# Batch 0's first two chunks store their score blocks unturned, and later chunks fetch and turn them

## The chip, the cores and the metric

One core of a Trainium2 chip runs the whole program. The metric is the device time of one execution in microseconds (us). The kernel before takes 2275.74 us, the median of three runs (2274.81 to 2275.78).

## The reference, cut to what matters

For each of 8 batches (3200 rows; `u` and `v` are 3200x256, `z` is 3200x64, all float32):

```python
scores = (1.0 / S) * np.matmul(z, z.transpose(0, 2, 1))
attn = np.maximum(scores, 0.0) ** 2
x = u * np.matmul(attn, v)
# xp: x with 4 rows of zeros ahead; K = 5
for k in range(K):
    gate_pre += conv_w[k] * xp[:, k:k + S, :]
out = (sigmoid(gate_pre) * (x @ w_val)) @ w_out
```

The matrix of scores is z times its own transpose, so it is symmetric: a block computed once is, turned over its diagonal, also the block at the mirrored place.

## The kernel before, in words

The 3200 rows of a batch are 25 tiles of 128. Queries go in 7 chunks `c` of 4, 4, 4, 4, 3, 3, 3 tiles (the last batch differs a little), and keys in 13 pairs of tiles `i` (the last pair is one tile). A step is one chunk against one pair, so a batch has 91 steps. `place[b, c, i]` says at which of a chunk's 13 places a pair is taken.

**One block.** A float32 product is made of three passes over a high and a low part (`hi`, `lo`, both fp32r). For a computed block TensorE (PE) makes the scores into a PSUM tile `s` of which there are two (`scores`, six 64-row matmuls, two at a time, recorded at L394). ScalarE (ACT) then does Relu (L589), Square (L590) and the cast to `ah` (L592, the high part), and VectorE (DVE) the rest `al` = a - ah (L598). PE multiplies `ah` and `al` with the values `v_hl` into `acc` (`attend`, L394 and L642). All this is written three steps ahead (`AHEAD = 3`): in step s PE makes the scores for step s + 3 in its middle, and ACT and DVE make the weights of s + 3.

**Mirrored blocks.** `keeps(b, c, g)` says whether the block of query chunk c and key chunk g > c is kept. If so, DVE turns it in 32x32 squares (`turn`, L468) into a tile `turned`, and `keep` stores it with four transfers into the DRAM tensor `mir`. When chunk g comes to the pairs of chunk c, `m_fetch` (L505) brings the block back into one of four buffers `m`, and only cast and rest are left: no scores, no Relu, no Square. In batch 0 chunk 0 is not kept at all, and chunk 1 only for g of 5 and 6. In the other batches every block with c < g is kept. `MIRRORED_AT` spreads the fetched pairs over the places of a chunk by their number.

**Order of the work.** Nothing is scheduled by the compiler: each engine takes its instructions in the order in which the Python loop over steps writes them. `at_step(s, fn, ...)` puts loads and side work (convolution, gate, value and out projections, conversion of the float64 weights) at a step. SyncE's queue (SP) issues all transfers in the same written order, and an issue that has to wait holds up those behind it. The transfers take eight semaphores (`DMAHW0` to `DMAHW7`) in turn, and a transfer waits until the one that had its semaphore before, eight issues earlier, has landed. Batch 0 starts with nothing on the core: while its chunk 0 is computed, SP loads `z`, all of `v`, the weights and `u` for batch 0 (`z_load`, `v_load0`, `v_load_chunk`, `u_load`).

**Buffers.** `a` has two tiles, `m` four, `turned` two, `v_raw` two. The float64 conversions (`convert_conv`, `convert`) take their scratch from `m` in the first chunks.

Of the kernel before, what the change touches and what calls it, by code (L numbers as in the profile page):

```python
# [7 lines left out]
F32 = mybir.dt.float32  # L8
# [4 lines left out]
P = 128  # L13
# [4 lines left out]
def attn_glu_kernel(  # L18
# [66 lines left out]

    def from_float64(dst, rest, raw, split, **kw):

        lo_w, hi_w = raw[..., 0], raw[..., 1]
        cols = 1
        for n in dst.shape[1:]:  # L90
            cols *= n
        ws = [sb.tile([P, 2, cols], U32, name=f"cv_words{i}", tag="m", bufs=4) for i in range(2)]
        ex, sc, mant, frac = (w[:, i, :].rearrange(split, **kw) for w in ws for i in range(2))
        ts, tt = nc.vector.tensor_scalar, nc.vector.tensor_tensor
        yield
        ts(ex, hi_w, 20, 0x7FF, op0=ALU.logical_shift_right, op1=ALU.bitwise_and)
# [24 lines left out]
        yield
        tt(dst, mant.bitcast(F32), rest, op=ALU.add)
# [20 lines left out]
    def convert(name):  # L143
        hi = const.tile([P, DH, D], F32R, name=f"w_{name}_hi")
        lo = const.tile([P, DH, D], F32R, name=f"w_{name}_lo")
        both = sb.tile([P, 2, DH, D], F32, name="w_f32", tag="m", bufs=4)
        wf, rest = both[:, 0], both[:, 1]
        yield from from_float64(wf, rest, w_raw[name], "p (h d) -> p h d", d=D)
        if name == "out":
# [137 lines left out]
    def keeps(b, c, g):  # L287

        return c < g and (b > 0 or c > 1 or (c == 1 and g >= 5))

# [168 lines left out]
    def turn(b, c, i, a):  # L459

        w = all_sizes[b][c] * P
        for j, g, t, m in runs(b, i):
            if keeps(b, c, g):
                size = all_sizes[b][g]
# [8 lines left out]
        if two_pairs(b, c) and i == own(b, c, 0):  # L473
# [20 lines left out]
    def m_fetch(b, c, i):  # L494
# [40 lines left out]
    def second_block(a, hi, lo, s):  # L535
        each = a.shape[1] // 2
        for j in range(2):
# [7 lines left out]
            rest(lo[:, x], a[:, x], hi[:, x])  # L545

    def weights_of(b, c, i):

# [5 lines left out]
        if halves(b, c, i) or split(b, c, i):  # L554
# [22 lines left out]
            return rests  # L577
        if mirrored(b, c, i):
            a = m_in.pop((b, c, i))[:, : n * w].rearrange("p (a j x) -> p a j x", a=P // BLK, j=n)
            hi, lo = (x.rearrange("p (j a x) -> p a j x", a=P // BLK, j=n) for x in (hi, lo))  # L580
        else:
            s = st_.pop((b, c, i))
            a = sb.tile([P, 2 * CW], F32, name="a", bufs=2)[:, : n * w]
            each = n * w // 2
            if b == c == 0 and i < 2:
                at[b, c, i] = (ah, al)
                first_block(a, hi, lo, s) if i == 0 else second_block(a, hi, lo, s)
                return lambda: None
            nc.scalar.activation(a.rearrange("p (j x) -> p j x", j=2), s[:, :, :each], AF.Relu, scale=scale)  # L589
            nc.scalar.activation(a, a, AF.Square)  # L590
        if cast_on_scalar(b, c, i):
# [5 lines left out]
        def rest():  # L597
# [4 lines left out]
            if not mirrored(b, c, i):  # L602
                if c == 1 and two_pairs(b, c) and i == own(b, c, 0) and place[b, c, i] == 0:
                    return lambda: turn(b, c, i, a)
                turn(b, c, i, a)

# [415 lines left out]
    for b in range(B):  # L1022
        for c in range(n_chunks):
# [39 lines left out]
            for i in range(NP):  # L1063
                if mirrored(b, c, i) or halves(b, c, i) or split(b, c, i):
                    at_step(s0 + place[b, c, i] - AHEAD - FETCH, m_fetch, b, c, i, first=True)
        if b == 0:
# [7 lines left out]
        else:  # L1074
            s1 = start(b - 1, n_chunks - 1)
            for i, p in enumerate(V_HIGH[b > 1]):
                at_step(s1 + p, v_high, b, i)
                at_step(s1 + p + 1, v_low, b, i)
            for p, tiles in V_LOAD[b > 1]:
                at_step(s1 + p, v_load, b, tiles)  # L1080
# [10 lines left out]
    with tc.manual_schedule():  # L1091
# [7 lines left out]
        for s in range(min(todo), END + 1):  # L1099
# [169 lines left out]
```

## Time and profile before

| what | before |
|---|---|
| median of 3 runs | 2275.74 us |
| span of the profiled execution (its own time has no row) | 2270.9 us |
| around the span, by the median | 4.8 us |
| PE, PEld busy | 2263.4, 2017.6 us |
| DVE, ACT busy | 1846.1, 1758.2 us |
| share of 16 DMA engines, queue q1 | 70.3% |
| chunk 0 of batch 0, 0 to 55.4 us | 55.4 us |
| chunks 1 to 6 of batch 0 | 46.6, 49.3, 46.2, 36.2, 33.6, 36.1 us |
| chunks 1 to 6 of batch 2 | 45.9, 44.3, 43.4, 33.9, 31.6, 34.3 us |

A chunk is taken from one `x<-acc,ut` product (L672), which ends a chunk's attention, to the next. Lines of a timeline give start, duration, engine, line of the kernel, operation, output<-inputs, and in brackets how long the engine was idle before and what released it. PE's matmuls overlap, so a group's own duration is longer than the distance to the next group's start; distances between starts are what PE takes.

### The profile page before, as it was taken

The numbers are of one execution on the slowest core, as the hardware profiler recorded it, in microseconds if no ns is written. First come the engines' busy times: TensorE is split into PE (matmuls) and PEld (weight loads), VectorE is DVE, ScalarE is ACT, GpSimd is POOL, SyncE is SP. The second block draws the span as 40 slices with busy tenths as digits, with TensorE's granted clock in tenths as the row PEclk, the third lists the DMA queues.
The fourth block names the chain that finished last, engine by engine and source line by source line (L and its number), as shares of the span: only waits on it lengthen the run. The fifth ranks groups of instructions, "written<-read, shape, count | busy, mean of one in ns | idle before, by whom it ended". The sixth has DMA issues, their size and how long they took to land.

```text
span 2270.9 us, 52418 instructions
## 1 busy us (share of the span) xinstructions
PE 2263.4 (100%) x21229; PEld 2017.6 (89%) x21229; DVE 1846.1 (81%) x2427; ACT 1758.2 (77%) x2326; POOL 65.3 (3%) x110
## 2 busy tenths in 40 slices
PE   9999999999999999999999999999999999999999
PEld 7889988899888998889988899888998889998889
DVE  7877798887988778887798878888788887788776
ACT  8987789766987669876698776986769876697755
POOL 0000000000000000000000000000000000000000
PEclk9999999999999999999999999999999999999999
DMA  5255776778667786677867778677687786877753
GB/s 119 44 119 117 178 172 156 178 168 212 157 159 177 164 221 160 157 174 167 211 157 168 179 169 195 157 177 175 159 200 164 182 173 156 197 170 177 194 145 97
DMA packets 691651, 374.96 MB, mean 165 GB/s; under 512 B 399312, under 2 KB 662992, under 8 KB 691408
## 3 DMA queue, kind: packets, MB, share of 16 engines
q1 hardware_dynamic: 690208, 371.35, 70.3%
q8 instruction: 166, 2.72, 0.5%
q14 instruction: 77, 0.63, 0.1%
q10 hardware_dynamic: 1200, 0.26, 0.1%
HBM read 205.86 MB, written 165.61 MB: 164 GB/s over the span
## 4 chain that ended last, share of the span: by engine, by line
PE 99%; DVE 0%; issue 0%; ACT 0%; DVEq 0%
PE acc L394 68%; PE s L394 11%; PE misc L394 10%; PE acc L642 8%; PE misc L834 1%; PE misc L758 1%; PE misc L401 0%; PE acc L834 0%; PE s L758 0%; DVE x L672 0%; DVE gvl L780 0%; DVE zhl L244 0%; DVE turned L478 0%; DVE a L527 0%; PE misc L214 0%
## 5 line engine op out<-in xcount | busy, mean ns | idle before, releaser
L394 PE MATMUL acc<-ah,v_hl 64*128 64x512 f32 (+1 forms) x9800 | 1543.2, 370 | 0.5 <-DVE ah L529 0.5
L394 PEld LDWEIGHTS acc<-ah,v_hl 64*128 64x128 f32 x9800 | 927.3, 185 | 120.6 <-issue 1.4
L394 PE MATMUL acc<-al,v_hl 64*128 64x512 f32 (+1 forms) x4900 | 921.6, 369 | 0.0
L598 DVE TENSOR_TENSOR al<-a,ah 128x1024 fp32r<-128x1024 f32 (+4 forms) x386 | 421.7, 1093 | 225.0 <-ACT ah L592 218.4
L394 PEld LDWEIGHTS acc<-al,v_hl 64*128 64x128 f32 x4900 | 469.2, 185 | 60.0 <-DVE al L516 0.9
L589 ACT ACTIVATE a<-s 128x1024 f32<-128x1024 f32 (+4 forms) x386 | 354.1, 917 | 160.9 <-PE s L394 147.9
L590 ACT ACTIVATE a<-a 128x1024 f32<-128x1024 f32 (+4 forms) x386 | 370.2, 959 | 12.2
L592 ACT CAST ah<-m 128x768 fp32r<-128x768 f32 (+2 forms) x303 | 269.1, 892 | 127.4 <-DMA m<-mir 52.4
L592 ACT CAST ah<-a 128x1024 fp32r<-128x1024 f32 (+3 forms) x351 | 334.5, 953 | 11.5
L598 DVE TENSOR_TENSOR al<-m,ah 128x768 fp32r<-128x768 f32 (+2 forms) x303 | 308.0, 1019 | 40.3 <-ACT ah L592 39.3
L468 DVE STREAM_TRANSPOSE turned<-a 128x1024 f32<-128x1024 f32 (+3 forms) x318 | 319.5, 1010 | 1.3 <-DMA mir<-turned 0.7
L713 DVE SCALAR_TENSOR_TENSOR gate<-x,cw,gate 128x512 f32<-128x512 f32 (+2 forms) x448 | 304.5, 680 | 4.4 <-ACT gate L711 0.3
L394 PE MATMUL s<-zq,zhl 64*128 64x512 f32 (+3 forms) x1722 | 231.9, 372 | 0.0
L394 PEld LDWEIGHTS s<-zq,zhl 64*128 64x128 f32 x1722 | 161.3, 185 | 23.1
L642 PE MATMUL acc<-ah,v_hl 128*128 128x384 f32 (+2 forms) x700 | 177.8, 332 | 0.2 <-DVE x L672 0.2
L672 DVE TENSOR_TENSOR x<-acc,ut 128x512 f32<-128x512 f32 (+2 forms) x112 | 65.8, 628 | 85.0 <-PE acc L394 55.4
L642 PEld LDWEIGHTS acc<-ah,v_hl 128*128 128x128 f32 x700 | 124.7, 188 | 4.6 <-issue 1.8
L642 PE MATMUL acc<-al,v_hl 128*128 128x384 f32 (+2 forms) x350 | 115.6, 330 | 0.0
L718 ACT ACTIVATE gate<-gate 128x512 f32<-128x512 f32 (+2 forms) x112 | 65.6, 585 | 58.2 <-DVE gate L713 58.1
L775 ACT CAST gvh<-gv 128x512 fp32r<-128x512 f32 (+2 forms) x112 | 64.0, 572 | 47.6 <-DVE gv L771 47.5
L771 DVE TENSOR_TENSOR gv<-misc,gate 128x512 f32<-128x512 f32 (+1 forms) x110 | 69.5, 632 | 15.1 <-PE misc L394 8.1
L711 ACT ACTIVATE gate<-x,cw 128x512 f32<-128x512 f32 (+2 forms) x111 | 74.8, 674 | 2.6 <-DVE x L672 2.6
(139 smaller groups left out, 1978.1 us busy)
## 6 DMA issues: line engine op xcount, KB each, us to landing
m<-mir SPq DMA_DIRECT2D x191, 384.0 KB, 5.1
mir<-turned SPq DMA_DIRECT2D x340, 192.0 KB, 3.3
mir<-turned SPq DMA_DIRECT2D x188, 256.0 KB, 4.0
m<-mir SPq DMA_DIRECT2D x94, 512.0 KB, 5.2
u_raw<-in_u_dram SPq DMA_DIRECT2D x264, 64.0 KB, 3.7
v_raw<-in_v_dram SPq DMA_DIRECT2D x116, 128.0 KB, 4.7
mir<-turned SPq DMA_DIRECT2D x84, 144.0 KB, 2.5
out_dram<-ob SPq DMA_DIRECT2D x92, 128.0 KB, 2.8
```

Of the source, the lines that this page charges most:

```text
L394: ins = nc.tensor.matmul(out_, st[r], mv[r], start=first, stop=last)
L468: nc.vector.transpose(into[:, t : t + m], a[:, j * w : (j + m) * w].rearrange("p (t m x) -> p t m x", t=m, x=BLK))
L589: nc.scalar.activation(a.rearrange("p (j x) -> p j x", j=2), s[:, :, :each], AF.Relu, scale=scale)
L590: nc.scalar.activation(a, a, AF.Square)
L592: nc.scalar.copy(hi, a)
L598: nc.vector.tensor_tensor(lo, a, f32(hi), op=ALU.subtract)
L642: nc.tensor.matmul(out_, st, mv, start=first, stop=last)
L672: nc.vector.tensor_tensor(x[:, h, HALO : HALO + w], accs[b, c][h][:, :w], ut[b, c][:, h, :w], op=ALU.mult)
L711: (first or nc.scalar.mul)(g, tap, cw[:, h, 0:1])
L713: nc.vector.scalar_tensor_tensor(g, tap, cw[:, h, k : k + 1], g, op0=ALU.mult, op1=ALU.add)
L718: nc.scalar.activation(g, g, AF.Sigmoid)
L771: nc.vector.tensor_tensor(gv[:, :w], pvs[b, c][e][:, :w], gates[b, c][:, e, :w], op=ALU.mult)
```

## The change

In batch 0 the blocks of chunks 0 and 1 are kept too (`keeps` is now `c < g` everywhere). They are not turned when they are made. Their `a` tile comes from the four `m` buffers in place of the two `a` buffers, the Relu writes it in strips of 64 columns of both tiles, and `keep_as_is` stores it from there with one transfer per key chunk into a DRAM tensor `raw`, in pieces of 512 or 256 bytes. A later chunk fetches such a block one step earlier than other blocks, with four transfers of 128 or 96 KB, and `turn_in` turns it on DVE one step ahead of the cast, into an `a` tile. With this, batch 0's chunks have the same fetched pairs as the other batches' (10 more blocks of 4 tiles' width, 8 more of 3), and `place` follows `MIRRORED_AT` for these numbers. Blocks of chunk 1 with g of 5 and 6, turned before they were stored until now, are stored unturned too. The two large conversions take their scratch from `v_raw` and `turned` in place of `m`; the conversion of the convolution's weights keeps its scratch in `m`. The loads and casts of batch 1's values go to the places that the other batches use.

```diff
-    def from_float64(dst, rest, raw, split, **kw):
+    def from_float64(dst, rest, raw, split, ws=None, **kw):
...
-        ws = [sb.tile([P, 2, cols], U32, name=f"cv_words{i}", tag="m", bufs=4) for i in range(2)]
+        ws = ws or [sb.tile([P, 2, cols], U32, name=f"cv_words{i}", tag="m", bufs=4) for i in range(2)]
...
-        both = sb.tile([P, 2, DH, D], F32, name="w_f32", tag="m", bufs=4)
+        both = sb.tile([P, 2, DH, D], F32, name="w_f32", tag="v_raw", bufs=2)
...
+        words = sb.tile([P, 2, 2, DH * D], U32, name="cv_words", tag="turned", bufs=2)
...
-        return c < g and (b > 0 or c > 1 or (c == 1 and g >= 5))
+        return c < g
+
+    def as_is(b, c):
+
+        return b == 0 and c < 2
...
-            if keeps(b, c, g):
+            if keeps(b, c, g) and as_is(b, c):
+                to_keep.append((b, c, g, a, j, t, m))
+            elif keeps(b, c, g):
...
+    def keep_as_is(b, c, g, a, j, t, m):
+
+        y = 2 * BLK
+        if (b, c, g) not in mirror:
+            mirror[b, c, g] = dram.tile([P, 2 * P // BLK, all_sizes[b][g] * y], F32, name=f"raw{c}_{g}", bufs=1)
+        nc.sync.dma_start(
+            mirror[b, c, g][:, :, t * y : (t + m) * y],
+            a.rearrange("p (z x) -> p z x", z=2 * P // BLK)[:, :, j * y : (j + m) * y],
+        )
...
+        if turns_in(b, c, i):
+            raw = mirror[b, i // 2, c].rearrange("(k r) (a h) x -> h a r k x", r=BLK, h=2)[i % 2]
+            into = mt[:, : P // BLK * n * y].rearrange("p (k x) -> p k x", k=P // BLK)
+            for a in range(P // BLK):
+                nc.sync.dma_start(into[a * BLK : (a + 1) * BLK], raw[a])
+            return
...
+    def turn_in(b, c, i):
+
+        n, w = pairs[i][1], all_sizes[b][c] * P
+        raw = m_in.pop((b, c, i))[:, : n * w]
+        a = turned_in[b, c, i] = sb.tile([P, 2 * CW], F32, name="a", bufs=2)[:, : n * w]
+        nc.vector.transpose(
+            a.rearrange("p (t m r) -> p t m r", t=2, r=BLK), raw.rearrange("p (m t r) -> p t m r", t=2, r=BLK)
+        )
...
-            a = sb.tile([P, 2 * CW], F32, name="a", bufs=2)[:, : n * w]
...
+            kept = as_is(b, c) and keeps(b, c, all_homes[b][k][0])
+            a = sb.tile([P, 2 * CW], F32, name="a", **(dict(tag="m", bufs=4) if kept else dict(bufs=2)))[:, : n * w]
...
+            if kept and n == 2:
+                raw, a, hi, lo = a, *by_strips(a, hi, lo)
+                s = s[:, :, :w].rearrange("p j (z x) -> p j z x", x=2 * BLK)
+                nc.scalar.activation(a, s, AF.Relu, scale=scale)
+                nc.scalar.activation(raw, raw, AF.Square)
...
-                    at_step(s0 + place[b, c, i] - AHEAD - FETCH, m_fetch, b, c, i, first=True)
+                    at_step(s0 + place[b, c, i] - AHEAD - FETCH - turns_in(b, c, i), m_fetch, b, c, i, first=True)
...
-            for i, p in enumerate(V_HIGH[b > 1]):
+            for i, p in enumerate(V_HIGH[1]):
...
-            for p, tiles in V_LOAD[b > 1]:
+            for p, tiles in V_LOAD[1]:
...
+            if ahead and s + AHEAD + 1 < N and turns_in(*steps[s + AHEAD + 1]):
+                turn_in(*steps[s + AHEAD + 1])
```

Where the instructions stand now is shown at two places. The first is SP's queue while chunk 0 of batch 0 is computed; `v_raws` are values, `z_raw` the rows of z, and the brackets name what an issue waits for. Before:

```order
L331 DMA v_raws<-in_v_dram 32x4x256 [waits DMAHW5_49]
L173 DMA z_raw<-in_z_dram 32x12x32 [waits DMAHW6_49,DVE_49]
L173 DMA z_raw<-in_z_dram 32x12x32 [waits DMAHW7_49]
L173 DMA z_raw<-in_z_dram 32x12x32 [waits DMAHW0_49]
L173 DMA z_raw<-in_z_dram 32x12x32 [waits DMAHW1_49]
L331 DMA v_raws<-in_v_dram 32x3x256 [waits DMAHW2_49]
L331 DMA v_raws<-in_v_dram 32x3x256 [waits DMAHW3_49]
```

And after the change, from the same transfer on (`raw_1`, `raw_2` are the stores of pairs 2, 3 and 4):

```order
L337 DMA v_raws<-in_v_dram 32x4x256 [waits DMAHW5_49]
L494 DMA raw_1_308<-a 1024x1x128 [waits DMAHW6_49,Activation_49]
L494 DMA raw_1_308<-a 1024x1x128 [waits DMAHW7_49,Activation_49]
L494 DMA raw_2_360<-a 1024x1x128 [waits DMAHW0_49,Activation_49]
L175 DMA z_raw<-in_z_dram 32x12x32 [waits DMAHW1_49,DVE_49]
L175 DMA z_raw<-in_z_dram 32x12x32 [waits DMAHW2_49]
L175 DMA z_raw<-in_z_dram 32x12x32 [waits DMAHW3_49]
L175 DMA z_raw<-in_z_dram 32x12x32 [waits DMAHW4_49]
L337 DMA v_raws<-in_v_dram 32x3x256 [waits DMAHW5_49]
L337 DMA v_raws<-in_v_dram 32x3x256 [waits DMAHW6_49]
L337 DMA v_raws<-in_v_dram 32x3x256 [waits DMAHW7_49]
L337 DMA v_raws<-in_v_dram 32x3x256 [waits DMAHW0_49]
```

Three stores now stand ahead of the rows of z for chunk 6, and the last three issues of this piece wait for the stores' own semaphores 6, 7 and 0 again.

The second place is ACT's queue in the same stretch: the Relu, Square and cast of pairs 5, 6 and 7. Before:

```order
L589 ACTIVATE a<-s 128x1024 [waits DVE_49,PE_49]
L590 ACTIVATE a<-a 128x1024 [waits Activation_49]
L592 CAST ah<-a 128x1024 [waits Activation_49]
L239 CAST zhl_396<-zz 128x384 [waits DVE_49]
L589 ACTIVATE a<-s 128x1024 [waits PE_49]
L590 ACTIVATE a<-a 128x1024 [waits Activation_49]
L592 CAST ah<-a 128x1024 [waits Activation_49]
```

And after:

```order
L641 ACTIVATE a<-s 128x2x8x64 [waits DMAHW6_49,DVE_49,PE_49]
L642 ACTIVATE a<-a 128x1024 [waits Activation_49]
L648 CAST ah<-a 128x1024 [waits Activation_49]
L241 CAST zhl_401<-zz 128x384 [waits DVE_49]
L641 ACTIVATE a<-s 128x2x8x64 [waits DMAHW7_49,PE_49]
L642 ACTIVATE a<-a 128x1024 [waits Activation_49]
L648 CAST ah<-a 128x1024 [waits Activation_49]
L241 CAST zhl_461<-zz 128x384 [waits DVE_49]
L641 ACTIVATE a<-s 128x2x8x64 [waits DMAHW0_49,PE_49]
```

The Relu of pairs 5, 6 and 7 now waits for the semaphores 6, 7 and 0, those of the three stores above: it writes into the `m` buffers that these stores read. Further on the Relu of pair 8 waits in the same way for the store of pair 6, that of pair 9 for pair 7's, that of pair 10 for pair 8's, and that of pair 11 for pair 10's, since the convolution's conversion holds part of the `m` buffers until step 9.

More of the change, by code (lines that the diff above doesn't have):

```diff
@@ L145, in convert @@
         lo = const.tile([P, DH, D], F32R, name=f"w_{name}_lo")
-        both = sb.tile([P, 2, DH, D], F32, name="w_f32", tag="m", bufs=4)
+        both = sb.tile([P, 2, DH, D], F32, name="w_f32", tag="v_raw", bufs=2)
         wf, rest = both[:, 0], both[:, 1]
-        yield from from_float64(wf, rest, w_raw[name], "p (h d) -> p h d", d=D)
+        words = sb.tile([P, 2, 2, DH * D], U32, name="cv_words", tag="turned", bufs=2)
+        ws = [words[:, i] for i in range(2)]
+        yield from from_float64(wf, rest, w_raw[name], "p (h d) -> p h d", ws=ws, d=D)
         if name == "out":
@@ L479, in turn @@
             to_keep.append((b, c, c))
+    def keep_as_is(b, c, g, a, j, t, m):
[6 more added lines that the diff above has]
+        )
     def keep():
         while to_keep:
+            if len(to_keep[0]) > 3:
+                keep_as_is(*to_keep.pop(0))
+                continue
             b, c, g = to_keep.pop(0)
@@ L545, in second_block, with by_strips, turns_in @@
             rest(lo[:, x], a[:, x], hi[:, x])
+    turned_in = {}
+    def turn_in(b, c, i):
[5 more added lines that the diff above has]
+        )
+    def by_strips(a, *both):
+        strips = a.rearrange("p (z j x) -> p j z x", j=2, x=2 * BLK)
+        return strips, *(y.rearrange("p (j z x) -> p j z x", j=2, x=2 * BLK) for y in both)
+    def turns_in(b, c, i):
+        return mirrored(b, c, i) and i < 4 and as_is(b, i // 2)
     def weights_of(b, c, i):
@@ L577, in weights_of @@
             return rests
-        if mirrored(b, c, i):
+        if turns_in(b, c, i):
+            a = turned_in.pop((b, c, i))
+        elif mirrored(b, c, i):
             a = m_in.pop((b, c, i))[:, : n * w].rearrange("p (a j x) -> p a j x", a=P // BLK, j=n)
@@ L588, in weights_of @@
                 return lambda: None
-            nc.scalar.activation(a.rearrange("p (j x) -> p j x", j=2), s[:, :, :each], AF.Relu, scale=scale)
-            nc.scalar.activation(a, a, AF.Square)
+            if kept and n == 2:
[3 more added lines that the diff above has]
+                nc.scalar.activation(raw, raw, AF.Square)
+            else:
+                nc.scalar.activation(a.rearrange("p (j x) -> p j x", j=2), s[:, :, :each], AF.Relu, scale=scale)
+                nc.scalar.activation(a, a, AF.Square)
+                raw = a
         if cast_on_scalar(b, c, i):
@@ L603, in rest @@
                 if c == 1 and two_pairs(b, c) and i == own(b, c, 0) and place[b, c, i] == 0:
-                    return lambda: turn(b, c, i, a)
-                turn(b, c, i, a)
+                    return lambda: turn(b, c, i, raw)
+                turn(b, c, i, raw)
         return rest
```

## The prediction

> **What bounds the kernel now.** I read the page's first lines, the chain that ended last, PE's timeline in batch 0, then busy time by stage. From the page:
>
> ```profile
> span 2270.9 us, 52418 instructions
> PE 2263.4 (100%) x21229; PEld 2017.6 (89%) x21229; DVE 1846.1 (81%) x2427; ACT 1758.2 (77%) x2326; POOL 65.3 (3%) x110
> PE 99%; DVE 0%; issue 0%; ACT 0%; DVEq 0%
> ```
>
> PE has work in all but 7.5 us of the span and makes 99% of the chain. So each matmul taken out is a gain, and each wait put in a loss, unless something else absorbs it. The stages of batch 0 beside those of batch 2 (columns: length, busy time of PE, PEld, DVE, ACT, POOL, granted clock, DMA share, GB/s) are chunks 3 and 4, then batch 0's chunk 6:
>
> ```profile
> 151.20:197.40 46.20, 46.20 (x417) 38.33 (x415) 33.31 (x40) 37.33 (x45) 1.24 (x2) 1.00 0.46 104
> 719.00:762.40 43.40, 43.40 (x394) 36.15 (x392) 34.93 (x43) 31.60 (x40) 2.08 (x2) 1.00 0.85 185
> 197.40:233.60 36.20, 36.20 (x408) 35.21 (x406) 27.56 (x36) 28.23 (x39) 0.97 (x2) 1.00 0.45 93
> 762.40:796.30 33.90, 33.90 (x384) 32.91 (x382) 28.03 (x38) 22.05 (x35) 0.97 (x2) 1.00 0.62 134
> 267.20:303.30 36.10, 34.93 (x412) 34.01 (x408) 30.17 (x47) 26.91 (x44) 2.15 (x2) 1.00 0.93 198
> PE misc L394 <- DVE gvl L780: 1.2, 1, 1.2
> ```
>
> Batch 2 has four fetched blocks more in each of chunks 3 and 4, and is 2.8 and 2.3 us shorter: the whole effect of a fetched block is 0.70 us at four tiles' width and 0.575 at three. In batch 0's chunk 6 PE is idle for 1.2 us, once, for `gvl` (last line, from the waits).
>
> **What it removes.** The new order has scores for 10 blocks fewer of four tiles' width and 8 fewer of three, all in chunks 1 to 6 of batch 0, where PE never rests: 10 x 0.70 + 8 x 0.575 = 11.6 us. With as many fetched blocks as other batches, chunk 6 leaves the spread pattern and runs as theirs, which show no such idle stretch; I take half of the 1.2, so 12.2 in all (11.0 to 12.8). ACT loses 18 Relus and 18 Squares there, which were off the path.
>
> **What it adds to DVE.** 22 turns at the cast, against 4 that go from chunk 1:
>
> ```profile
> L468 DVE STREAM_TRANSPOSE turned<-a 128x1024 f32<-128x1024 f32 x179 | 221.6, 1238 | 0.7 <-DMA mir<-turned 0.5
> L468 DVE STREAM_TRANSPOSE turned<-a 128x768 f32<-128x768 f32 x21 | 20.4, 971 | 0.0
> 303.30:348.90 45.60, 45.60 (x424) 39.69 (x424) 42.09 (x55) 42.74 (x55) 0.10 (x1) 1.00 0.71 175
> ```
>
> In chunk 3 DVE gets 4 x 1.24 = 5.0 us and comes to 38.3 of some 43.4; in chunk 4 it gets 4 x 0.97 and comes to 31.4 of 33.9, 93%. The stretch quoted last, with DVE at 42.1 of 45.6 (92%), kept PE busy throughout, so I take 0.5 us for all turns (0 to 3). Fetching takes four issues in place of one, three more at about 0.5 us of SP each, in chunks where the DMA share is 0.46; the fetch is issued three steps ahead of its turn. Nothing.
>
> **What it adds in chunk 0.** Here 11 blocks are stored, 5.4 MB, some ten transfers of 512 KB between loads that run back to back. The queue of SP, ACT's Relus of pairs 5, 8 and 11, the rests of the same pairs, and PE's scores in the middle of steps 4 and 5:
>
> ```profile
> 22.57 1.89 SPq L331 DMA_DIRECT2D v_raws<-in_v_dram  x4
> 24.55 1.92 SPq L173 DMA_DIRECT2D z_raw<-in_z_dram  x4
> 26.52 3.77 SPq L331 DMA_DIRECT2D v_raws<-in_v_dram  x8
> 30.34 0.43 SPq L133 DMA_DIRECT2D w_val_raw<-in_moe_w_val_dram  x1
> 22.13 1.02 ACT L589 ACTIVATE a<-s 128x1024 f32<-128x1024 f32 x1
> 23.18 1.06 ACT L590 ACTIVATE a<-a 128x1024 f32<-128x1024 f32 x1
> 25.64 1.02 ACT L589 ACTIVATE a<-s 128x1024 f32<-128x1024 f32 x1
> 32.26 1.02 ACT L589 ACTIVATE a<-s 128x1024 f32<-128x1024 f32 x1
> 35.77 1.02 ACT L589 ACTIVATE a<-s 128x1024 f32<-128x1024 f32 x1
> 38.87 1.01 ACT L589 ACTIVATE a<-s 128x1024 f32<-128x1024 f32 x1
> 41.97 1.02 ACT L589 ACTIVATE a<-s 128x1024 f32<-128x1024 f32 x1
> 25.36 1.22 DVE L598 TENSOR_TENSOR al<-a,ah 128x1024 fp32r<-128x1024 f32 x1
> 35.48 1.22 DVE L598 TENSOR_TENSOR al<-a,ah 128x1024 fp32r<-128x1024 f32 x1 [0.31 <-ACT ah L592]
> 45.20 1.23 DVE L598 TENSOR_TENSOR al<-a,ah 128x1024 fp32r<-128x1024 f32 x1 [0.65 <-ACT ah L592]
> 27.18 0.86 PE L394 MATMUL s<-zhl,zhl 64*128 64x512 f32 x6
> 27.88 0.39 PE L394 MATMUL acc<-ah,v_hl 64*128 64x512 f32 x2
> 30.64 0.86 PE L394 MATMUL s<-zhl,zhl 64*128 64x512 f32 x6
> 20.00:30.00 10.00, 10.00 (x90) 8.12 (x89) 9.74 (x18) 9.81 (x12) 0.00 (x0) 1.00 0.72 155
> ```
>
> A step takes 30.64 - 27.18 = 3.46 us. Between two scores lie two halves of (30.64 - 27.88) / 2 = 1.38 us, so step 5 starts at 29.26 and needs `al` one pair of matmuls later (1.38 / 6 = 0.23), at 29.5. The rest of pair 5 ends at 26.6: 2.9 us of slack. For pair 8 it is 39.9 against 36.7 (3.2), for pair 11, behind the half-size scores of pair 12, 49.9 against 46.4 (3.5).
>
> Now the stores. SP issues without a pause up to 24.55, and only there comes the store of pair 2, whose Square was long done. The Relu of pair 5 writes into the buffer that this store reads, so it can't start at 22.13 any more. No store in 512-byte pieces is in the trace; the nearest rows:
>
> ```profile
> m<-mir SPq DMA_DIRECT2D x94, 512.0 KB, 5.2
> w_val_raw<-in_moe_w_val_dram SPq DMA_DIRECT2D x1, 512.0 KB, 3.8
> v_raws<-in_v_dram SPq DMA_DIRECT2D x8, 128.0 KB, 3.0
> v_raws<-in_v_dram SPq DMA_DIRECT2D x8, 96.0 KB, 2.6
> 260.00:284.00 24.00, 24.00 (x290) 24.00 (x288) 18.07 (x28) 18.51 (x31) 0.79 (x1) 1.00 0.97 206
> ```
>
> 512 KB land after 3.8 to 5.2 us. Behind each other they take at least what w_val takes beyond a 96 KB load (1.2 us for 416 KB, so 1.5), and at most what the fullest stretch allows (524 KB at 206 GB/s: 2.5). I take 2.1 apart, nearer the upper end since the engines are 0.72 busy with small pieces there, and 4.65 for the first, of which 0.8 is receipt.
>
> 1. Stores of pairs 2, 3, 4 land at 29.2, 31.3, 33.4. Relu 5 starts at 29.2, 7.1 late: less 2.9, PE is 4.2 us late at step 5. Relus 6 and 7 follow 3.5 apart (25.64 - 22.13, with a cast of `zhl` between), at 32.7 and 36.2, after their stores.
> 2. Relu 8 waits for the store of pair 6. SP reaches it late, because a load before it waits for the semaphore of pair 4's store (33.4) and eight more issues of 0.47 follow. Ahead of it on the engines from 32.6 on are 192 KB of z, 768 KB of v, pair 5's store and w_val, 1984 KB, at 2.1 us per 512 KB 8.1 us: until 40.7. It lands at 40.7 + 2.1 + 0.8 = 43.6. Relu 8 is 11.3 late, less 3.2: PE is 8.1 late.
> 3. Relus 9 and 10 follow at ACT's pace (3.5 and 3.1), 47.1 and 50.2. Relu 11 waits for the store of pair 10, which needs its Square (52.3) and stands behind pair 9's store and some `u` until 53.4: 53.4 + 2.1 + 0.8 = 56.3. It is 14.3 late, less 3.5: PE is 10.8 us late at step 11.
>
> Nobody gives this back, as PE is the bound after it. In chunk 1, before the change,
>
> ```profile
> 56.00:101.90 45.90, 45.81 (x388) 37.27 (x388) 40.22 (x57) 43.95 (x51) 1.34 (x2) 1.00 0.28 56
> ```
>
> the DMA share is 0.28, and every Relu there waits for a store at least two computed blocks back: nothing. The same three steps with 1.5 apart and 3.8 for a landing give 5.8 us, where only ACT's old pace after a late Relu 5 and the landing of pair 10's store are left; with 2.5 and 5.2 they give 13.8. That is some 8 us of loss for each us apart.
>
> A restart may also be slow. The kernel's first 13 matmuls of 512 columns:
>
> ```profile
> 1.45 5.56 PE L401 MATMUL misc<-zeros 128*128 128x512 f32 x13 [1.45 <-DVE zeros L1093]
> ```
>
> 5.56 / 13 = 0.43 us each, against 0.23 later, at a granted clock of 1.00 in the rows. The longest wait in my list is 3.0 us (from 27.18 until Relu 5 ends at 30.2). I add nothing. The Trainium skill (TensorE: Matmul & The Clock Gate, Part 1) says that a window of about 3.4 us without work halves the clock for about another; no stretch of this trace tests it in mid-kernel. By it a wait that came out somewhat longer would cost 1.7 us more, each time, and the sum would be 2276.5 with one.
>
> **The sum.** Against the profiled execution: 2270.9 - 12.2 + 10.8 + 0.5 = 2270.0 of span; the median is 4.8 us above the span, so 2275.74 - 0.9 = **2274.8 us**, no change that can be measured: 0.2%, or 4.6 us, is about what a measurement of this kernel can tell.
>
> **The rivals.**
>
> *The stores land early* (chance 0.30). If the first lands within 3.8 us and the others 1.5 apart, the loss is 5.8: 2275.74 - 12.2 + 5.8 + 0.5 = 2269.8. It decides from about 1.65 apart on down, where the loss falls under 7.2; if buffers never made anyone wait the time would be 2264.0. For it speaks w_val's 3.8 in the same stretch; against it that the first store can't be issued before 24.55, 2.4 us after its Relu wanted the buffer, and the 0.72 share. The Trainium skill (DMA: Bandwidth & Descriptors, Anatomy of one DMA) gives 2.0 us and bytes over 436 GB/s; by that a store would land after 3.2 and take 1.2 of the engines, and the sum, by ACT's pace and one landing, would be 2268.4. The fetches' 5.2 us disagree.
>
> *The DMA engines become the bound of chunk 0* (0.20). The place is steps 2 and 3 above. At 512 bytes a store is 1024 pieces, and the fetches show that bytes alone don't set the time:
>
> ```profile
> m<-mir SPq DMA_DIRECT2D x191, 384.0 KB, 5.1
> ```
>
> These take as long as those of 512 KB, in as many pieces. If a store takes 3.2 us, the loss is 10.8 + 1.1 x 8 = 19.6, and the kernel takes 2283.6. It decides from about 2.8 apart, where the loss passes 16.3. Against it: the engines reached 206 GB/s at 0.97.
>
> *DVE becomes the bound of chunks 2 to 6* (0.04). All turns on the path would cost 10 x 1.24 + 12 x 0.97 = 24 us, 2298 with chunk 0's 10.8. It decides where DVE has no idle time left over a chunk; 93% is the most that comes out above.
>
> That the change doesn't do what it says is excluded: the scores are gone from the order.
>
> **How the numbers follow.** The forecast case, waits worth 7.2 to 16.3 us, has the remaining 0.46 and is all "same" (2271.2 to 2280.3). Faster has the first rival's 0.30, slower 0.20 + 0.04. The range from 2268 to 2282 holds the bounds of the store's cost (2269.8 to 2277.8), a little more at the lower end for removals of up to 12.8 and earlier landings, and at the upper end half of the second rival; some 2 in 10 are left out.
>
> **What would show it.** In the profile after: 108 fewer score matmuls; Relus of pairs 5, 8 and 11 idle before, released by a transfer `raw<-a`; PE with about 11 us of waits before 66 us, on ACT or DVE, and none after; chunk 0 about 66 us long, chunks 1 to 6 about 12 us shorter together; stores landing 4 to 5 us after issue. The prediction is wrong if chunk 0 stays at 55 to 61 us (stores are quicker), exceeds 73 (the transfers bind), or if chunks 2 to 6 have waits of PE on DVE.

## The result and the profile after

The changed kernel takes 2297.74 us (median of 4 runs, 2294.05 to 2298.43) against 2275.27 us for the kernel before in the same session: ratio 1.0094, interval 1.0080 to 1.0109. It is 22.5 us slower, where 0.9 us less was forecast and 2282 was the upper end of the range. The page of the changed kernel begins, and its chain of waits reads:

```profile
span 2296.1 us, 52032 instructions
PE 2266.3 (99%) x20965; PEld 1993.6 (87%) x20965; DVE 1864.8 (81%) x2446; ACT 1724.1 (75%) x2289; POOL 65.5 (3%) x110
PE 84%; DMA 5%; DVE 5%; ACT 3%; SPq 2%; issue 2%; DVEq 0%; ACTq 0%
```

PE now has 29.8 us without work, 22.3 more than before, and the chain is no longer all PE: transfers, DVE and ACT hold parts of it. Where that is, the windows of batch 0's seven chunks say (length; busy time of PE, PEld, DVE, ACT, POOL; granted clock; DMA share; GB/s):

```profile
0.00:68.33 68.33, 57.12 (x420) 45.71 (x422) 43.15 (x84) 46.10 (x53) 0.75 (x7) 0.98 0.76 185
68.33:115.46 47.13, 45.58 (x382) 36.08 (x380) 39.86 (x59) 41.20 (x48) 1.34 (x2) 1.00 0.62 143
115.46:163.86 48.40, 47.50 (x420) 39.36 (x418) 41.51 (x48) 32.22 (x41) 1.25 (x2) 1.00 0.65 156
163.86:211.95 48.09, 44.96 (x386) 40.32 (x384) 36.79 (x44) 32.53 (x39) 2.17 (x2) 0.96 0.69 164
211.95:246.88 34.93, 34.59 (x384) 33.19 (x382) 31.14 (x42) 19.56 (x30) 0.98 (x2) 1.00 0.58 128
246.88:283.52 36.64, 34.10 (x357) 33.27 (x354) 29.30 (x41) 20.97 (x33) 1.57 (x2) 0.95 0.64 160
283.52:323.75 40.23, 37.30 (x301) 34.68 (x299) 32.55 (x52) 25.82 (x41) 2.62 (x2) 1.00 0.95 194
```

Batch 0 takes 323.75 us against 303.31, 20.4 more: chunk 0 12.9, chunks 1 to 5 together 3.4 (215.2 against 211.8, though 11.6 less 0.5 for the turns was forecast as a gain, all of it here, as the rows of the score matmuls below show), chunk 6 4.1. DVE is busy for 41.5 of 48.4 us in chunk 2 and 36.8 of 48.1 in chunk 3, so it is not full, yet PE waits there; the granted clock falls to 0.96 and 0.95 in chunks 3 and 5. The other seven batches take 1972.4 us against 1967.6; the kernels below, e3 apart, have 1967.4 to 1971.8 there, mostly by the lengths of their chunks 6, so I don't put these 4.8 us down to the change.

**Chunk 0.** ACT's queue has three waits for stores, at the three Relus that were named (timeline; start, duration, then the operation, in brackets the idle time before and its releaser):

```profile
28.33 1.02 ACT L641 ACTIVATE a<-s 128x1024 f32<-128x1024 f32 x1 [5.61 <-DMA raw<-a]
43.52 1.03 ACT L641 ACTIVATE a<-s 128x1024 f32<-128x1024 f32 x1 [4.99 <-DMA raw<-a]
57.24 1.02 ACT L641 ACTIVATE a<-s 128x1024 f32<-128x1024 f32 x1 [3.91 <-DMA raw<-a]
```

**Chunks 1 to 5.** The waits of the whole span name a new pair, ACT's cast for DVE's turn:

```profile
ACT ah L648 <- DVE a L581: 46.1, 20, 4.5
ACT a L641 <- DMA raw<-a: 14.5, 3, 5.6
```

One of these 20 waits, in chunk 3, shown on ACT, then on DVE, then on PE (not every line of the stretch):

```profile
171.79 1.05 ACT L648 CAST ah<-a 128x1024 fp32r<-128x1024 f32 x1
176.53 1.05 ACT L648 CAST ah<-a 128x1024 fp32r<-128x1024 f32 x1 [3.06 <-DVE a L581]
...
172.87 1.23 DVE L654 TENSOR_TENSOR al<-a,ah 128x1024 fp32r<-128x1024 f32 x1 [2.29 <-ACT ah L648]
174.02 1.30 DVE L476 STREAM_TRANSPOSE turned<-a 128x512 f32<-128x512 f32 x2
175.24 1.20 DVE L581 STREAM_TRANSPOSE a<-m 128x1024 f32<-128x1024 f32 x1
179.22 1.18 DVE L654 TENSOR_TENSOR al<-a,ah 128x1024 fp32r<-128x1024 f32 x1
...
177.63 0.50 PE L400 MATMUL acc<-ah,v_hl 64*128 64x512 f32 x2 [0.43 <-ACT ah L648]
180.46 0.50 PE L400 MATMUL acc<-al,v_hl 64*128 64x512 f32 x2 [2.33 <-DVE al L654]
```

DVE idles 2.29 us for a cast of ACT; then come the rest of that pair, the turn of that pair for later chunks, and only then the turn of the fetched block (L581). ACT's next cast needs that turn and idles 3.06 us. The two engines take turns at waiting for each other: a ring of cast, rest, turn, turn in, cast. While ACT makes the late cast, DVE has gone on to side work (`xl`, `ob` and `ut`, from 176.36 to 179.3), so the rest of the fetched pair starts only at 179.22, and PE waits 2.33 us for it. The wait of ACT just before this one is 3.15 us (at 164.03); that these two and the side work together use up the three steps of lead is my reading.

### The profile page after: what moved, and what is told of

The parts are those of the page before. It is cut to its first block, busy times and chain, and to the rows that moved or that the text cites. A ratio compares the mean times of both kernels' runs of the same rounds, so it can differ in the third digit from the quotient of the medians.

```text
span 2296.1 us, 52032 instructions
## 1 busy us (share of the span) xinstructions
PE 2266.3 (99%) x20965; PEld 1993.6 (87%) x20965; DVE 1864.8 (81%) x2446; ACT 1724.1 (75%) x2289; POOL 65.5 (3%) x110
## 3 DMA queue, kind: packets, MB, share of 16 engines
q8 instruction: 164, 2.69, 0.5%
## 4 chain that ended last, share of the span: by engine, by line
PE 84%; DMA 5%; DVE 5%; ACT 3%; SPq 2%; issue 2%; DVEq 0%; ACTq 0%
PE acc L400 58%; PE s L400 9%; PE misc L400 9%; PE acc L698 6%; DMA v_raw<-in_v_dram 2%; DMA m<-mir 1%; DVE al L654 1%; ACT ah L648 1%; SPq L175 1%; PE misc L890 1%; SPq L337 1%; PE misc L814 1%; ACT a L645 1%; DVE a L581 1%; ACT a L644 1%
## 5 line engine op out<-in xcount | busy, mean ns | idle before, releaser
L400 PE MATMUL acc<-ah,v_hl 64*128 64x512 f32 (+1 forms) x9632 | 1515.2, 371 | 11.9 <-DVE v_hl L387 4.5
L400 PEld LDWEIGHTS acc<-ah,v_hl 64*128 64x128 f32 x9632 | 904.1, 184 | 144.3 <-ACT ah L648 6.4
L400 PE MATMUL acc<-al,v_hl 64*128 64x512 f32 (+1 forms) x4816 | 905.4, 371 | 8.3 <-DVE al L654 7.7
L654 DVE TENSOR_TENSOR al<-a,ah 128x1024 fp32r<-128x1024 f32 (+3 forms) x390 | 425.1, 1090 | 232.1 <-ACT ah L648 225.6
L644 ACT ACTIVATE a<-s 128x1024 f32<-128x1024 f32 (+3 forms) x350 | 319.4, 912 | 142.0 <-PE s L400 133.2
L654 DVE TENSOR_TENSOR al<-m,ah 128x768 fp32r<-128x768 f32 (+2 forms) x299 | 304.1, 1019 | 48.1 <-ACT ah L648 46.8
L645 ACT ACTIVATE a<-a 128x1024 f32<-128x1024 f32 (+3 forms) x350 | 333.7, 953 | 11.1
L698 PE MATMUL acc<-ah,v_hl 128*128 128x384 f32 (+2 forms) x784 | 199.5, 332 | 0.2 <-DVE x L728 0.2
L698 PEld LDWEIGHTS acc<-ah,v_hl 128*128 128x128 f32 x784 | 139.8, 188 | 4.9 <-issue 2.1
L698 PE MATMUL acc<-al,v_hl 128*128 128x384 f32 (+2 forms) x392 | 129.6, 330 | 0.3 <-DVE al L654 0.3
L382 ACT CAST v_hl<-v_raw 128x512 fp32r<-128x512 f32 (+1 forms) x92 | 55.3, 601 | 33.3 <-DMA v_raw<-in_v_dram 33.3
```

Of the source, the lines that this page charges most:

```text
L400: ins = nc.tensor.matmul(out_, st[r], mv[r], start=first, stop=last)
L654: nc.vector.tensor_tensor(lo, a, f32(hi), op=ALU.subtract)
L698: nc.tensor.matmul(out_, st, mv, start=first, stop=last)
```

## The experiments

The chunk lengths of batch 0 in each profile, and the medians against the kernel before in the same session:

| run | chunk 0 | chunks 1 to 5 | chunk 6 | batch 0 | median us | ratio (interval) |
|---|---|---|---|---|---|---|
| before | 55.4 | 211.8 | 36.1 | 303.3 | 2275.3 | |
| the change | 68.3 | 215.2 | 40.2 | 323.8 | 2297.7 | 1.0094 (1.0080 to 1.0109) |
| turn first (e1) | 69.7 | 203.3 | 44.2 | 317.2 | 2287.5 | 1.0053 (1.0038 to 1.0068) |
| no turns (e2) | 68.2 | 200.0 | 43.3 | 311.5 | 2282.6 | 1.0032 (1.0021 to 1.0043) |
| scratch off m (e3) | 61.3 | 216.6 | 40.4 | 318.3 | 2308.3 | 1.0147 (1.0132 to 1.0162) |
| in place (e4) | 68.2 | 215.3 | 40.1 | 323.6 | 2293.6 | 1.0083 (1.0068 to 1.0098) |
| scratch, aligned (e5) | 61.6 | 212.5 | 42.2 | 316.3 | 2287.1 | 1.0053 (1.0038 to 1.0068) |
| e1 + early z (e6) | 68.1 | 205.0 | 36.1 | 309.1 | 2281.2 | 1.0030 (1.0020 to 1.0040) |
| e1 + e5 + early z (e7) | 60.8 | 205.3 | 38.9 | 305.0 | 2274.9 | 0.9998 (0.9989 to 1.0008) |
| chunk 1 alone, e1 (e8) | 55.2 | 208.3 | 37.8 | 301.3 | 2274.8 | 0.9998 (0.9989 to 1.0008) |
| e7, stores on ACT (e9) | 67.9 | 203.0 | 36.6 | 307.4 | 2281.7 | 1.0032 (1.0020 to 1.0045) |
| e9 without 0 to 6 (e10) | 69.4 | 205.9 | 38.0 | 313.4 | 2285.6 | 1.0046 (1.0032 to 1.0060) |
| e7, stores on POOL (e11) | 56.3 | 204.6 | 37.8 | 298.7 | 2271.7 | 0.9986 (0.9977 to 0.9995) |
| e11, turn before side work (e12) | 56.6 | 204.9 | 36.6 | 298.1 | 2271.3 | 0.9983 (0.9974 to 0.9993) |

**1. The turn first in DVE's queue (e1).**

```diff
+            if ahead and s + AHEAD + 1 < N and turns_in(*steps[s + AHEAD + 1]):
+                turn_in(*steps[s + AHEAD + 1])
             if late:
                 held.append(weights_of(*late))
...
-            if ahead and s + AHEAD + 1 < N and turns_in(*steps[s + AHEAD + 1]):
-                turn_in(*steps[s + AHEAD + 1])
```

> The turn of a fetched block is written in DVE's queue ahead of the rest and turn of the step before it instead of behind them, and is made in place in its m buffer (no second a tile was free). Loop theory (the cast of ACT waits for a turn that stands behind a rest that waits for ACT's cast before): chunks 1 to 6 lose most of their 19 us above the forecast, 2280 to 2286 in all, and ACT's waits on the turns fall from 46 us to under 15. DVE-capacity theory (DVE has no room for 24 us of turns): the same DVE work, so 2295 to 2300. Transfer theory (the fetches land late): 2295 to 2300, with waits of the turns on the fetches.

Measured 2287.47 us, 10.3 less, just outside the 2280 to 2286 of the loop theory and far from the rivals' 2295 to 2300. Chunks 1 to 5 fell by 11.9 us with the same DVE work, and the waits on the turns to:

```profile
ACT ah L647 <- DVE m L581: 10.2, 9, 1.7
```

So it was order and not capacity. The expectation counted chunk 6 with the turns, and that was wrong: it grew from 40.2 to 44.2. Chunk 5 is 3.1 us shorter in e1, and more of the transfers around it fall into chunk 6 (packets under 5).

**2. The turns left out (e2).** `turn_in` isn't called and the fetched block is cast as it lies, so these blocks' weights are not the right ones; only the time is read.

> The 22 turns at the cast are left out: ACT casts the fetched block as it lies, so the weights of these blocks are wrong numbers and only the time counts. Loop theory: chunks 1 to 6 come down by 14 to 19 us, 2279 to 2284. DVE-capacity theory: the same 2279 to 2284, but then turning first must not reach it. Transfer theory: the fetches are as many and as late as before, so 2294 to 2299.

Measured 2282.60 us, as the loop theory said. The windows of its chunks:

```profile
68.23:113.31 45.08, 44.99 (x382) 36.26 (x380) 37.67 (x56) 40.99 (x48) 1.34 (x2) 1.00 0.65 150
113.31:158.88 45.57, 45.41 (x412) 37.18 (x410) 35.66 (x44) 35.45 (x45) 2.08 (x2) 1.00 0.68 166
158.88:202.36 43.48, 43.48 (x394) 36.06 (x392) 32.49 (x39) 29.54 (x36) 2.08 (x2) 1.00 0.72 172
202.36:236.40 34.04, 34.04 (x384) 33.03 (x382) 27.68 (x37) 21.59 (x33) 0.97 (x2) 1.00 0.63 145
236.40:268.19 31.79, 31.79 (x353) 31.24 (x350) 23.94 (x35) 19.57 (x32) 1.54 (x2) 1.00 0.70 177
268.19:311.49 43.30, 38.88 (x305) 35.20 (x303) 31.78 (x49) 24.88 (x41) 2.61 (x2) 1.00 0.91 184
```

In chunks 1 to 5 PE waits almost nowhere, and they take 11.9 us less than before the change: that is what the fetched blocks are worth, and the fetches themselves delay nobody there. So the turns cost 215.2 - 200.0 = 15.2 us, of which turning first gives back 11.9. Chunk 6 is as long as in e1, so its loss has nothing to do with turns.

**3. The scratch off the m buffers (e3), and the same at aligned addresses (e5).**

```diff
-        rest = sb.tile([P, DH, KW], F32, name="cv_rest", tag="m", bufs=4)
+        rest = sb.tile([P, DH, KW], F32, name="cv_rest", tag="cv", bufs=3)
```

The two `cv_words` tiles move in the same way; in e5 each of the three is 64 words wide in place of 20.

> The scratch of the convolution's conversion (240 bytes a partition) leaves the m buffers, so all four take turns as the a tiles of chunk 0. Buffer theory: Relus 8 and 11 have their buffer one store earlier and pair 5 finds one free; PE's 11 us of waits in chunk 0 fall to 0 to 3 and the kernel takes 2285 to 2289. Transfer theory (the DMA engines at a share of 0.76 hold chunk 0): the stores and loads are the same, the gain is under 3 us, 2295 to 2298.

> As the run with the convolution's scratch off the m buffers, but each of the three scratch tiles takes 256 bytes a partition in place of 80, so that all tiles behind them start at multiples of 256 bytes again. Address theory (240 bytes of new tiles moved the others, and the matmuls of 512 columns took 0.228 in place of 0.224 us each): the pace is 0.224 again, chunk 0 keeps its 7 us, 2288 to 2292. If the freed m buffers or the scratch themselves slowed the rest of the program: 2305 to 2311 as in that run.

e3 took 2308.34 us, 10.6 more, outside both theories. Chunk 0 did fall, by 7.1 us, but the four-tile chunks of the later batches grew, from 45.89 to 46.56 us in the usual one, while those of three tiles did not (33.95 and 33.97). It shows in PE's groups of one chunk of batch 1, first in e3, then in e5:

```profile
L400 PE MATMUL acc<-ah,v_hl 64*128 64x512 f32 x200 | 33.7, 390 | 0.0
```

```profile
L400 PE MATMUL acc<-ah,v_hl 64*128 64x512 f32 x200 | 33.3, 387 | 0.0
```

With three tiles of 80 bytes a partition ahead of the others, starts of matmuls lie 0.228 us apart; with 256 bytes each, 0.224 as before, and the kernel takes 2287.05, just under what the address theory expected. With the scratch moved, batch 0 is 7.4 us shorter, 6.7 of them in chunk 0; the rest of the 10.7 us between the medians lies in the later batches. Of its waits, those for `raw<-a` shrank to 3.13 and 0.21 us; one for `u`, whose loads stand behind the stores in SP's queue, is new (DVE turns `u` late, and PE waits for the `x` made with it):

```profile
62.36 0.50 PE L698 MATMUL acc<-ah,v_hl 128*128 128x512 f32 x1 [2.85 <-DVE x L728]
```

**4. The turn in place, not moved (e4).** e1 also turned in place, so this is its control.

> The turn stays where the change has it in DVE's queue, but is made in place in its m buffer, so the two a tiles serve only computed blocks. If the order in DVE's queue is the cause (loop theory): no change, 2295 to 2299. If Relus and turns wait for each other's a tiles: 2283 to 2290, as good as turning first.

Measured 2293.60 us, a little below what the order theory expected. By the trace nothing changed where the turns are: chunks 1 to 5 take 215.3 us and batch 0 is 0.2 us shorter than with the change; the rest of the difference lies in the later batches (1967.4 against 1972.4 us). A trap for readers is in its waits: the same wait of 3.06 us at the same place has another name.

```profile
176.29 1.05 ACT L647 CAST ah<-m 128x1024 fp32r<-128x1024 f32 x1 [3.06 <-PE acc L400]
...
175.01 1.20 DVE L581 STREAM_TRANSPOSE m<-m 128x1024 f32<-128x1024 f32 x1
```

The cast starts 0.08 us after the turn ends at 176.21, so it is the turn that it waited for. Sums of a waits view over such a change have to be held against the lengths of the chunks.

**5. z of batch 1 earlier (e6).**

```diff
-    Z_FROM = {b: (-12, -7, -1, 7, 17, 23, 37) if b > 1 else (22, 26, 3, 8, 17, 30, 36) for b in range(1, B)}
+    Z_FROM = {b: (-12, -7, -1, 7, 17, 23, 37) for b in range(1, B)}
```

> Turns first and in place, and z of batch 1 loaded at the steps that the later batches use, most of it before batch 0's chunk 6 (with chunks 0 and 1 kept, the high and low parts of z of their rows are free early). Transfer theory for chunk 6 (0.91 to 0.95 of the DMA engines, fetches landing 7 us after issue, four z loads that later batches have elsewhere): chunk 6 falls from 44.2 to 35 to 38 us, and the kernel takes 2279 to 2283. If the fetches and the values alone hold chunk 6: under 2 us of gain, 2285.5 to 2288.

Measured 2281.22 us, as the transfer theory said: chunk 6 fell from 44.2 to 36.1. The packets of the transfers in chunk 6, in the kernel before, with the change, in e1 and in e6:

```profile
DMA packets 17414, 7.15 MB, mean 198 GB/s; under 512 B 11058, under 2 KB 17409, under 8 KB 17409
```

```profile
DMA packets 19722, 7.79 MB, mean 194 GB/s; under 512 B 13242, under 2 KB 19719, under 8 KB 19719
```

```profile
DMA packets 21615, 8.19 MB, mean 185 GB/s; under 512 B 14860, under 2 KB 21612, under 8 KB 21612
```

```profile
DMA packets 14226, 7.13 MB, mean 198 GB/s; under 512 B 7727, under 2 KB 14223, under 8 KB 14223
```

Divided by the lengths (36.1, 40.2, 44.2, 36.1 us) these are 483, 490, 489 and 394 packets per us. In the first three the chunk is as long as its packets take, at one rate, though their bytes differ by 15%; in e6 most of the small pieces of z are gone, and PE is busy throughout:

```profile
273.00:309.07 36.07, 36.07 (x303) 35.26 (x303) 29.97 (x46) 24.67 (x40) 2.62 (x2) 1.00 0.82 198
```

So chunk 6 stood close to what the transfers allow before the change, where PE still filled it but for 1.2 us, and the change put 2300 packets more into it. The one rate points at the number of packets rather than the bytes; no run changed the size of the pieces alone, so this is not shown. Nor is it the fetches for chunk 6 themselves that fill it. SP's queue before the change, and with it from `m<-raw` on:

```profile
258.43 1.91 SPq L173 DMA_DIRECT2D z_raw<-in_z_dram  x4
262.81 1.86 SPq L490 DMA_DIRECT2D mir<-turned  x4
...
270.05 3.67 SPq L527 DMA_DIRECT2D m<-raw  x8
281.53 2.07 SPq L175 DMA_DIRECT2D z_raw<-in_z_dram  x4
284.73 1.93 SPq L511 DMA_DIRECT2D mir<-turned  x4
```

The sixteen fetches of its four unturned blocks are issued from 270.05 to 280.5, all in chunk 5. Four loads of z and four stores of turned blocks stand behind them in the queue: they were issued 8.8 and 4.4 us ahead of chunk 6 (which began at 267.23) and now come 2.0 us ahead of it and 1.2 us into it (it begins at 283.52), and their packets fall into chunk 6. Why e7 and e11 stand at 38.9 and 37.8 there, at 390 and 396 packets per us, was not followed up.

**6. All three (e7), and chunk 1 alone (e8).** e8 has `c < g and (b > 0 or c > 0)` in `keeps`.

> The three together: turns first and in place, z of batch 1 early, the convolution's scratch off the m buffers at aligned addresses. If the three costs are separate they add: 2287.5 less 7 less 6 to 8, 2272 to 2275, level with the kernel before. If the transfers moved out of chunk 6 or the earlier stores meet others in chunks 0 to 5: 2276 to 2282.

> Chunk 0 of batch 0 is not kept, as before the change; chunk 1 is kept unturned, and its blocks are turned first and in place. Six blocks are fetched that the kernel before computed, worth 4 x 0.70 + 2 x 0.575 = 4.0 us. If the stores of chunk 0 are the cost that can't be hidden: chunk 0 is back at 55.4, and the kernel takes 2270 to 2274. If fetching unturned blocks costs as much by itself (turns, late transfers in chunk 6): 2275 to 2281.

e7 took 2274.86 us, level with before, as the sum of three separate costs said. e8 took 2274.80, between its two ranges: chunk 0 is back at 55.2, but of the 4 us that its six blocks are worth 3.5 are left after chunk 5, and chunk 6 takes 1.7 of them.

**7. The stores from other queues (e9, e10, e11).** In e9 `keep_as_is` uses `nc.scalar.dma_start`, in e11 `nc.gpsimd.dma_start`; e10 is e9 with `(b, c, g) != (0, 0, 6)` in `keeps`, and z of batch 1's chunk 0 loaded in chunk 6 again.

> All three changes, and the stores of unturned blocks are issued by ACT right behind their Squares, not by SP between its loads. Queue theory (what is left of chunk 0's loss, 60.8 against 55.4 us, is that SP reaches the stores late and then the u loads late behind them): the first store is issued at 18 to 20 us in place of 24.2, u lands before 55 us, chunk 0 takes 56 to 58 us and the kernel 2270 to 2273. If the 5.4 MB on the DMA engines are the cost: chunk 0 stays at 60 to 61, 2274 to 2276. If ACT's own time (11 issues) counts: over 2276.

> As that, but the two blocks of chunk 0 that chunk 6 would fetch are neither stored nor fetched; chunk 6 makes their scores itself, 2 x 0.575 = 1.15 us of PE. Transfer theory for chunk 6 (38.9 us where later batches take 34.2 to 35): 768 KB less at some 195 GB/s are 3.9 us of transfers, so chunk 6 comes to 35 to 37 us, 1 to 3 us less in all than the run with everything kept. If chunk 6 is held by something else: it stays at 39 or grows by 1.15, and the kernel takes 0 to 1.5 us more.

> All three changes, and the stores of unturned blocks issued by POOL, which has next to nothing to do, in place of SP (in the run of 2274.9) or ACT (in the run of 2281.7, where chunk 0 took 67.9). Queue theory: no load on SP stands behind a store and no Relu on ACT behind an issue that waits for a semaphore, the u loads land before 55 us, chunk 0 takes 56 to 59 us and the kernel 2270 to 2273. If the 5.4 MB of stores cost the DMA engines' time by themselves: chunk 0 stays at 60 to 62, 2273 to 2277. If an issue by POOL takes much longer than SP's 0.5 us: stores land later, chunk 0 over 62, above 2277.

e9 took 2281.73 us, chunk 0 67.9: the queue theory's 56 to 58 was wrong for this queue, and over 2276 is the third case's number, though ACT lost most by waits and not by the issues' own 0.52 us each. An issue waits for the transfer that had its semaphore before, and on ACT that holds up the Relus behind it, now for loads that have nothing to do with them:

```profile
22.91 1.02 ACT L640 ACTIVATE a<-s 128x1024 f32<-128x1024 f32 x1 [4.08 <-DMA z_raw<-in_z_dram]
35.05 1.02 ACT L640 ACTIVATE a<-s 128x1024 f32<-128x1024 f32 x1 [5.44 <-DMA v_raws<-in_v_dram]
```

e10 took 2285.58 us and is no clean test: its z loads for batch 1's chunk 0 are back in chunk 6, which is 1.5 us longer than in e9 although it fetches less, and chunk 0, which differs by the stores of pairs 11 and 12, and chunk 5 are 1.5 and 2.9 us longer. At 3.9 us more than e9 it lies outside both cases; it doesn't support the transfer theory as put there, and can't refute it either.

e11 took 2271.74 us against 2273.91 for the kernel before in its session, as the queue theory said: 0.14% less, with an interval that ends just below 1. Chunk 0, and the stores' landing time:

```profile
0.00:56.27 56.27, 53.88 (x419) 44.66 (x421) 43.94 (x83) 46.66 (x54) 11.53 (x19) 1.00 0.88 225
```

```profile
raw<-a POOLq DMA_DIRECT2D x16, 512.0 KB, 4.6
```

The stores take no less time than SP's (3.8 us by the median), the engines are busier (0.88 against 0.76), and yet only 0.9 of the 12.9 us are left. So the loss of chunk 0 was the place of the stores and of what stands behind them in SP's queue, and m buffers held by scratch, not the 5.4 MB.

**8. The turn ahead of the side work (e12).** The two lines of e1 stand before the loop over `todo`.

> As the run with the stores on POOL, but the turn is written ahead of the step's side work too (the rest of x, the turn of u, gate sums), which stood before it in DVE's queue at the start of chunk 5, where ACT waited 1.96 us for a turn and PE 1.79 us. Loop theory: chunks 4 and 5 fall from 35.0 and 34.9 to 34.0 and 32 us, those of the run without turns; 2267 to 2270 in all. If the side work then comes too late for PE, or chunk 6 takes the gain back (its transfers have an end of their own): 2271 to 2273.

Measured 2271.34 us, no different from e11, and chunks 4 and 5 stayed at 35.0 and 34.9 (34.0 and 31.8 without turns). ACT's wait at that place shrank from 1.96 to 0.25 us, but the rest that PE needs now stood behind the side work: there DVE has more than one step's work, and order alone doesn't help. The rival of side work that comes too late for PE holds. In e11 and e12 the granted clock also fell once in chunk 5 (0.95 over the chunk in e11), which is part of what is left there.

## Why the prediction was wrong

**The turns at the cast: the failed step.** "So I take 0.5 us for all turns (0 to 3)" was argued from DVE's busy share staying under 93%. They cost 15.2 us, 2.7 of them through the granted clock (below). DVE had the time; what the step left out is that the turn makes ACT's cast of these blocks depend on DVE, where until then ACT ran ahead of DVE, and that it is written behind the rest that waits for ACT. The order of the changed kernel showed both; a busy share can't. e1 (same work, other place: -11.9 us in chunks 1 to 5) and e4 (other buffer, same place: none) show it. The rival of a full DVE, put at 24 us and to decide once DVE had no idle time left over a chunk, is not what happened. The last of the prediction's signs of being wrong, waits of PE on DVE in chunks 2 to 6, is what came: in chunks 1 to 5 PE waits 6.3 us for `al`.

**Chunk 6: also failed.** "Chunk 6 leaves the spread pattern and runs as theirs" was to give 0.6 us for an idle stretch. It lost 4.1. The row that I quoted for this chunk had a DMA share of 0.93, and I read only its PE column: the fetches in chunk 5 pushed other transfers into a stretch that had no room for them. e6, which takes loads of z out of it, shows that room was what was lacking. Even then the chunk takes 36.1 us with PE busy throughout, so it did not come to run as theirs (34.3 in batch 2).

**The removed scores: right.** 11.6 us were forecast; e2, which has nothing else in chunks 1 to 5, took 11.9 us less there. The prediction put the removed scores into chunks 1 to 6; all lie in 1 to 5, since scores are made three steps ahead. The score matmuls in the windows of chunks 1 to 6 were 82, 78, 66, 54, 30 and 32 and are now 70, 48, 42, 30, 12 and 32: 108 fewer, as forecast, and none of them in chunk 6 (its rows for tile `s`, before and after; columns as above without POOL):

```profile
267.23:303.31 36.08, 4.11 (x32) 2.90 (x32) 0.00 (x0) 4.33 (x5) 1.00 0.93 198
283.52:323.75 40.23, 4.24 (x32) 2.79 (x32) 0.00 (x0) 3.33 (x4) 1.00 0.95 194
```

**Chunk 0: right in mechanism and place, 2 us small.** The landings that end the three waits were put at 29.2, 43.6 and 56.3. Since an idle time of ACT ends with the landing, Relus 5, 8 and 11 (quoted above) place them at 28.3, 43.5 and 57.2. No row shows the 0.8 us of receipt that these sums use; the traces show only the whole time to landing, 3.8 us by the median. The loss was 12.9 for 10.8. What PE waited for last, at step 11, stands in DVE's queue behind the rest of pair 11 (DVE, then PE's waits in steps 8 and 11):

```profile
60.47 1.23 DVE L654 TENSOR_TENSOR al<-a,ah 128x1024 fp32r<-128x1024 f32 x1 [4.65 <-ACT ah L648]
61.62 0.68 DVE L387 TENSOR_TENSOR v_hl<-v_raw,v_hl 128x512 fp32r<-128x512 f32 x1
...
49.19 0.50 PE L400 MATMUL acc<-ah,v_hl 64*128 64x512 f32 x2 [2.24 <-ACT a L642]
62.45 0.51 PE L400 MATMUL acc<-ah,v_hl 64*128 64x512 f32 x2 [1.77 <-DVE v_hl L387]
```

It is the low part of the pair's values, `v_hl`. It ended at 47.02 before the change and at 62.30 after it, 15.3 us later, and the chunk lost 12.9: the slack was 2.4 us. The prediction sized it by the rest alone, at 3.5. So of the 2 us, 1.1 are the slack and 0.9 the later landing.

**The slow restart.** The prediction added nothing for it, and in chunk 0 that came out right, though for no reason that it gave. PE's windows around the first long wait, then after the ones in chunks 3 and 5:

```profile
31.50:34.40 2.90, 0.27 (x4) 0.00 (x0) 2.85 (x5) 2.84 (x5) 0.00 (x0) 1.00 0.78 181
34.40:38.20 3.80, 3.75 (x20) 3.43 (x22) 3.29 (x9) 3.74 (x5) 0.00 (x0) 0.57 0.88 242
...
182.50:185.50 3.00, 3.00 (x18) 2.34 (x16) 3.00 (x4) 0.33 (x1) 0.00 (x0) 0.57 0.96 167
...
260.30:263.20 2.90, 2.77 (x18) 2.77 (x20) 2.50 (x5) 0.83 (x1) 0.00 (x0) 0.50 0.69 218
```

After 2.9 us almost without work the granted clock is 0.57 for 3.8 us, a loss of 3.8 x 0.43 = 1.6 us of PE's time. The chunk doesn't show it: PE idles again later for 2.24 and 1.77 us (lines above), so it would only have waited longer. The Trainium skill (TensorE: Matmul & The Clock Gate, Part 1) names a window of about 3.4 us; the traces of the change agree with the price that the prediction took from it, 1.7 us each time, but not with the length of the wait: the longest single wait of PE ahead of this fall was 2.69 us. In chunks 3 and 5 the fall does count. There e5 has the same order and the same waits but a granted clock of 1.00, and takes 46.86 and 35.19 us for 48.09 and 36.64, together 2.7 us of what I count under the turns.

**The rivals for chunk 0.** Neither early stores nor DMA engines as the bound: the waits ended with the landings, and e11 carried the same bytes with 0.9 us of loss. The stores landed after 3.8 us by the median from SP's queue and 4.6 from POOL's, not after the 3.2 that the prediction worked out from the Trainium skill (DMA: Bandwidth & Descriptors, Anatomy of one DMA, whose figures are for transfers that GpSimd issues).

**The range.** It held the uncertain cost of the stores and half a rival; it held no case in which a term that I called nothing or 0.5 us became the largest. Chunk 0 and the removed scores alone would have left it at 2275.3 - 11.9 + 12.9 = 2276.3, well inside.

## What to carry to other kernels

When a new instruction puts one in-order engine ahead of another that it used to follow, walk round the ring of waits it closes, instruction by instruction, before looking at busy shares; write such an instruction ahead of those that wait for the other engine, where the engine has time left in those steps (e12 is a place where it hadn't). Put stores on a queue where nobody urgent stands behind them: with the m buffers free, the same 5.4 MB cost chunk 0 5.4 us from SP's queue, 12.5 from ACT's and 0.9 from POOL's (e7, e9, e11). And hold every stretch that receives new transfers, or transfers that new ones push back in the queue, against the work that is already there, by its count of packets too and not only its bytes.

## What the runs showed of the hardware that was not expected

- New tiles of 80 bytes a partition, three of them, slowed the 512-column matmuls of the whole program from 0.224 to 0.228 us: batches 1 to 7 take 1989.4 us in e3 and 1968.5 in e5, where the tiles have 256 bytes and the pace is back. Which operand's address matters wasn't tried.
- Chunk 6 moved 483 to 493 packets per us in five kernels (before, the change, e1, e2 and e5) whose bytes there ranged from 7.15 to 8.19 MB, and 467 in e8.
- The clock does not always fall: the pair of waits of 0.4 and 2.3 us in chunk 3 was followed by 0.57 in the changed kernel, and waits of 0.5 and 2.3 us by 1.00 in e5:

```profile
173.60:176.60 3.00, 2.89 (x24) 2.36 (x26) 3.00 (x5) 0.32 (x1) 0.00 (x0) 1.00 0.24 39
```
